# Second-layer weights: half of them converted in the fourth chunk, straight into their kept tiles

## Chip, cores and metric

One NeuronCore of a Trainium2 chip runs the whole program. The metric is device time in microseconds, taken from start to end of one execution; a run is repeated and the median is given. The execution that the profiler recorded has a time of its own.

## What is computed

Hash attention over two batches of 768 tokens with 8 heads of 64, then two feed-forward layers over the 1536 tokens (512 wide, 2048 hidden). Cut to what matters:

```python
# attention: a query sees only keys whose 6 hash bits (signs of q @ proj, k @ proj) are the same
scores = scale * q @ k.T;  scores = where(same_bucket, scores, -1e9)
x = softmax(scores) @ v                          # 1536 x 512 after the heads are joined
# first layer
h = maximum(x @ w_in1, 0.0);   x = (h * h) @ w_out1
# second layer
h = x @ w_in2;  g = maximum(h, 0.0) + alpha * minimum(h, 0.0)
out = g @ w_out2
```

The weights come to the chip as the bits of float64 numbers, 8 bytes each; the kernel makes float32 of them itself, and it splits every operand of a large product into a high and a low part (three products for one).

## The kernel before

The 1536 tokens are four chunks of 384. The program does the attention of chunk 0 alone. Then it goes through the first layer's chunks 0 to 3 and the second layer's chunks 0 to 3, each by `feed_forward(l, c, background)`, in 16 steps `f` over the hidden width. One step does `hidden` (12 matmuls of 384 columns, lines 665 to 667), the activation (lines 672 to 683, giving a high part `gh` and a low part `gl`) and `project` (9 matmuls of 512 columns, lines 693 to 697) for the step before. The attention of chunks 1 to 3 runs beside the first layer's chunks 0 to 2.

A *unit* `(l, f, o)` is one weight tile of 128 x 512: `o` is 0 for the matrix into the hidden width and 1 for that out of it, so a layer has 32 units. How a unit comes to TensorE:

- `load_bits` (lines 578 to 582) loads its 512 KB of float64 bits into a buffer `wide`.
- `to_f32` (584 to 599) makes float32: one ScalarE copy of the high word into `we` (line 591), and on VectorE two instructions that build sign and low bits in `wsg` (593, 594) and one that joins them (596). `we` and `wsg` have one buffer each. The result goes into the tile that is handed over, or else stays in `we`.
- `split_w` (612 to 619) makes the high part `wh` on ScalarE (617) and the low part `wl` on VectorE or GpSimd (618).

The first layer's units are converted in chunk 0 by `fetch` (631 to 649), written to DRAM, and fetched again in each later chunk. The second layer's 32 units are converted by `ahead` (601 to 605): `to_f32` without a tile, then a DMA of 256 KB from `we` to a DRAM tile `w_d[u]` (line 605). Later `keep` (607 to 610) loads each from DRAM into a tile of the pool `res` that stays until the end, so that the second layer fetches nothing. In that layer `fetch` finds a unit in `kept` and takes it from there (634, 635).

Work beside the feed-forward is a list of steps with marks: `Background` (554 to 568) is called at 80 slots of a chunk and runs as many steps as its marks ask for at that place, laid evenly between two marks. The list of `load_bits` and `ahead` has 64 steps between 1.0 and 2.9 chunks (lines 797 to 802), that is beside chunks 1 and 2 of the first layer. The list of `keep` has 32 steps between 0.25 and 1.3 chunks counted from the start of chunk 3 (819, 820). Chunk 3 begins after the attention's pools are closed and the weight pools opened again with more buffers (812 to 816): `wide` has three buffers before and eight after.

All these DMAs are issued by SyncE's queue in the order that the compiler fixed. The compiler places each engine's instructions by the order in which they were written and by its own reckoning of when their operands are ready, so an instruction can stand ahead of one that was written earlier.

Of the kernel before, what the change touches and what calls it, by code (L numbers as in the profile page):

```python
# [23 lines left out]
EVICT = ("aavaav", "avavav", "vvavva", "vvavva")  # L24

LEAD = 0.88


@with_exitstack
def kernel(  # L30
# [20 lines left out]
    nc = tc.nc  # L51
# [10 lines left out]
    KFF = w_in1.shape[0]  # L62
# [438 lines left out]
    def attention_beside():  # L501


        pairs = [Pair(c, j) for c in range(1, NCH) for j in range(NPAIR)]
        steps, ends = [], []

        def begin():
            if (1, 0) not in raw:
                load_pair(1, 0)

        def turn(pr, u):
            for a in range(2):
                steps.append(lambda a=a: pr.p_t(*divmod(u, NTB), a))

        def values(pr, part):
            steps.append(lambda: pr.av(part))

        def finish(pr):
            steps.append(pr.finish)
            if pr.j == NPAIR - 1:  # L520
                ends.append(len(steps))

        steps += [begin] + pairs[0].prepare()
        last = 2 * NTB - 1
        for n, pr in enumerate(pairs):
            old = pairs[n - 1] if n else None
            prep = pairs[n + 1].prepare() if n + 1 < len(pairs) else []
            for u in range(2 * NTB):
                steps.append(lambda pr=pr, u=u: pr.scores(*divmod(u, NTB)))
                if prep and u != 1:  # L530
                    steps.append(prep.pop(0))
                if u == 0 and old:
                    turn(old, last)
                    steps.append(old.recip)
                    values(old, 0)
                if u == 1 and old:
                    values(old, 1)
                    values(old, 2)
                if u:
                    turn(pr, u - 1)  # L540
                if u == 4 and prep:
                    steps.append(prep.pop(0))
                if u == (3 if old and old.j == NPAIR - 1 else last) and old:
                    finish(old)
            assert not prep
        turn(pr, last)
        steps.append(pr.recip)
        for part in range(3):
            values(pr, part)
        finish(pr)  # L550
        return steps, ends
# [22 lines left out]
    w_d = {}  # L574
    kept = {}
    y_d = {}

    def load_bits(u):
        l, f, o = u
        t = state["wide"].tile([P, DM, 2], U32, tag="wide", name="wbits")  # L580
        nc.sync.dma_start(out=t.rearrange("p n b -> p (n b)"), in_=(WO if o else WI)[l][f].bitcast(U32))
        w_bits[u] = t

    def to_f32(u, w=None):


        if u not in w_bits:
            load_bits(u)
        t = w_bits.pop(u)
        e = state["conv"].tile([P, DM], F32, tag="we", name="we")  # L590
        nc.scalar.activation(e, t[:, :, 1].bitcast(F32), AF.Copy, scale=2.0 ** -112)
        s = state["conv"].tile([P, DM], U32, tag="wsg", name="wsg")
        nc.vector.tensor_scalar(s, t[:, :, 1], 0x80000000, None, ALU.bitwise_and)
        nc.vector.scalar_tensor_tensor(s, t[:, :, 0], 29, s, ALU.logical_shift_right, ALU.bitwise_or)
        w = e if w is None else w
        nc.vector.scalar_tensor_tensor(  # L596
            w.bitcast(U32), e.bitcast(U32), 3, s, ALU.logical_shift_left, ALU.bitwise_or
        )
        return w

    def ahead(u):

        w = to_f32(u)
        w_d[u] = dram.tile([P, DM], F32, tag="w%d_%d_%d" % u, name="w%d_%d_%d" % u)
        nc.sync.dma_start(out=w_d[u], in_=w)

    def keep(u):

        kept[u] = state["res"].tile([P, DM], F32, name="w%d_%d_%d" % u)
        nc.sync.dma_start(out=kept[u], in_=w_d[u])  # L610

    def split_w(u, engine):
        w = w_f.pop(u)
# [142 lines left out]
    def second_x(c):  # L756

        cell = []

        def begin():  # L760
            new_x((1, c))
            y = state["res"].tile([P, NTB, DM], F32, tag="yb", name="yb")
            nc.sync.dma_start(out=y, in_=y_d[c])
            cell.append(y)

        def block(t):
            ps = ps_s.tile([P, 2, 512], F32, tag="s", name="s")[:, t % 2, :]
            for m in range(KDM):
                nc.tensor.transpose(ps[:, m * P:(m + 1) * P], cell[0][:, t, m * P:(m + 1) * P], ident)
            src = ps.rearrange("p (m n) -> p m n", m=KDM)  # L770
            xh, xl = xT[1, c]
            hi = xh[:, :, t * P:(t + 1) * P]
            nc.scalar.activation(hi, src, AF.Copy)
            nc.vector.tensor_tensor(xl[:, :, t * P:(t + 1) * P], src, f32(hi), ALU.subtract)

        return [begin] + [lambda t=t: block(t) for t in range(NTB)]
# [18 lines left out]
    steps, ends = attention_beside()  # L795
    following = Background(steps, [(0.0, 0)] + [(c + LEAD, n) for c, n in enumerate(ends)])
    steps = []
    for f in range(KFF):
        for o in range(2):
            steps += [lambda u=(1, f, o): load_bits(u), lambda u=(1, f, o): ahead(u)]  # L800

# [14 lines left out]
    state["attention"] = False  # L816


    steps = [lambda f=f, o=o: keep((1, f, o)) for f in range(KFF) for o in range(2)]
    conversion = Background(steps, [(0.25, 0), (1.3, len(steps))])  # L820
    for n in range(NCH + 1):
        steps = second_x(n) if n < NCH else []
# [76 lines left out]
```

## Time and profile before

| | us |
|---|---|
| three timed runs | 833.96, 840.73, 841.98 |
| their median | 840.73 |
| the profiled execution | 836.36 |
| its span, first to last instruction | 834.6 |
| TensorE matmuls busy in the span | 796.7 (95%) |
| VectorE busy | 499.6 (60%) |
| ScalarE busy | 472.4 (57%) |
| GpSimd busy | 360.8 (43%) |

The profiled execution is one run of the program; its span leaves out 1.8 us around the first and last instruction. Times below are in us from the span's start. In the rows PE is TensorE, PEld its weight loads, DVE VectorE, ACT ScalarE, POOL GpSimd, SP SyncE; L596 is line 596 of the kernel. Matmuls are pipelined and their ends are modelled, so an engine that is busy all the time may still be late. A "<-" behind an instruction names what ended the wait before it. The chain of waits is followed back from the last instruction to whatever released it.

### The profile page before, as it was taken

Reading aid. Unit: us, or ns where it says so; the run is one execution under the profiler, and the core shown is the slowest. Engines: PE = TensorE matmul, PEld = TensorE weight load, DVE = VectorE, ACT = ScalarE, POOL = GpSimd, SP = SyncE. Lnnn points to the kernel's source line nnn. Section 1 sums busy time; section 2 is a strip of 40 time slices with the busy share of each in tenths; the row PEclk is TensorE's granted clock in tenths of the full one; section 3 lists DMA queues with packets and bytes.
Section 4 is the critical chain, followed back from the end, with each engine's and each line's share of the span. In section 5 each row is a group of like instructions: output and inputs, shape, how many; then the busy total and the mean of one; then the engine's idle time right before and its main releaser. Section 6 shows DMA issues by size and latency. Waiting matters only on the chain.

```text
span 834.6 us, 12635 instructions
## 1 busy us (share of the span) xinstructions
PE 796.7 (95%) x4384; PEld 646.4 (77%) x4384; DVE 499.6 (60%) x822; ACT 472.4 (57%) x926; POOL 360.8 (43%) x321
## 2 busy tenths in 40 slices
PE   6999899999999999999999999999999999999997
PEld 4665667766777768668787789989988998998995
DVE  7678799978657648687797432234445444444442
ACT  5677677866656556656675466654444444443441
POOL 1002223332455556543333345555455555545553
PEclk9999999999999999999999999999999999999999
DMA  6757678877777776787774499500100001001001
GB/s 183 201 155 235 209 242 257 269 224 207 208 235 223 215 239 215 257 272 230 219 239 145 124 308 330 199 39 1 38 15 24 6 34 38 1 1 38 1 1 38
DMA packets 54864, 127.62 MB, mean 153 GB/s; under 512 B 7216, under 2 KB 11600, under 8 KB 54800
## 3 DMA queue, kind: packets, MB, share of 16 engines
q1 hardware_dynamic: 54800, 126.81, 48.9%
q8 instruction: 34, 0.56, 0.3%
q14 instruction: 30, 0.25, 0.1%
HBM read 82.93 MB, written 23.12 MB: 127 GB/s over the span
## 4 chain that ended last, share of the span: by engine, by line
PE 53%; DVE 4%; DMA 3%; ACT 3%; issue 2%; POOL 1%; POOLq 0%; DVEq 0%; SPq 0%; ACTq 0%
PE acc L697 8%; PE acc L693 8%; PE acc L694 7%; PE m L667 4%; PE m L665 4%; PE m L666 4%; PE h L665 4%; PE h L666 3%; PE h L667 3%; PE m L423 3%; DMA w<-we 2%; PE s L384 2%; PE m L407 2%; DVE we L596 1%; DVE low L389 1%
## 5 line engine op out<-in xcount | busy, mean ns | idle before, releaser
L683 POOL TENSOR_TENSOR gl<-g,gh 128x384 fp32r<-128x384 f32 x128 | 134.6, 1051 | 249.6 <-ACT gh L682 123.0
L693 PE MATMUL acc<-wh,gh 128*128 128x512 f32 x384 | 159.9, 416 | 0.0
L618 POOL TENSOR_TENSOR wl<-wf,wh 128x512 fp32r<-128x512 f32 x80 | 109.2, 1367 | 114.8 <-ACT wh L617 98.2
L694 PE MATMUL acc<-wl,gh 128*128 128x512 f32 x384 | 151.9, 396 | 0.0
L617 ACT ACTIVATE wh<-w 128x512 fp32r<-128x512 f32 x128 | 80.5, 629 | 80.9 <-PE m L666 44.6
L617 ACT ACTIVATE wh<-wf 128x512 fp32r<-128x512 f32 x128 | 80.2, 629 | 68.3 <-PE h L666 35.9
L697 PE MATMUL acc<-wh,gl 128*128 128x512 f32 x384 | 113.8, 396 | 1.8 <-POOL gl L683 1.8
L665 PE MATMUL h<-xh,wh 128*128 128x384 f32 x296 | 107.0, 361 | 2.5 <-ACT xh L451 1.6
L666 PE MATMUL h<-xl,wh 128*128 128x384 f32 x296 | 100.4, 339 | 0.6 <-POOL xl L452 0.6
L667 PE MATMUL h<-xh,wl 128*128 128x384 f32 x296 | 100.6, 340 | 0.0
L389 DVE TENSOR_REDUCE low<-s 128x1 f32<-128x768 f32 x84 | 79.9, 951 | 27.2 <-PE s L384 26.4
L392 ACT ACTIVATE sm<-s,low 128x768 f32<-128x768 f32 x84 | 75.5, 898 | 34.0 <-DVE low L389 33.5
L407 PE MATMUL m<-ident,sm 128*128 128x128 f32 x531 | 85.3, 276 | 3.8 <-ACT q L317 1.3
L384 PE MATMUL s<-k,q 128*128 128x384 f32 x336 | 79.7, 356 | 9.6 <-ACT sm L392 8.3
L697 PEld LDWEIGHTS acc<-wh,gl 128*128 128x128 f32 x384 | 71.9, 188 | 21.0 <-POOL gl L683 4.4
L618 POOL TENSOR_TENSOR wl<-w,wh 128x512 fp32r<-128x512 f32 x64 | 82.7, 1292 | 6.0 <-ACT wh L617 6.0
L693 PEld LDWEIGHTS acc<-wh,gh 128*128 128x128 f32 x384 | 72.2, 188 | 13.2 <-issue 3.1
L407 PEld LDWEIGHTS m<-ident,sm 128*128 128x128 f32 x531 | 65.2, 141 | 21.6 <-ACT q L317 2.5
L682 ACT ACTIVATE gh<-g 128x384 fp32r<-128x384 f32 x64 | 33.5, 524 | 81.6 <-DVE g L681 81.6
L680 DVE TENSOR_SCALAR r<-m,alpha_sb 128x384 f32<-128x384 f32 x43 | 26.5, 617 | 87.0 <-PE m L667 86.8
L384 PEld LDWEIGHTS s<-k,q 128*128 128x128 f32 x336 | 58.2, 192 | 26.4 <-ACT sm L392 16.1
L694 PEld LDWEIGHTS acc<-wl,gh 128*128 128x128 f32 x384 | 72.5, 189 | 7.7
(117 smaller groups left out, 1423.4 us busy)
## 6 DMA issues: line engine op xcount, KB each, us to landing
wf<-w SPq DMA_DIRECT2D x96, 256.0 KB, 3.0
wbits<-in_w_in_dram SPq DMA_DIRECT2D x32, 512.0 KB, 4.2
wbits<-in_w_out_dram SPq DMA_DIRECT2D x32, 512.0 KB, 4.3
q<-q SPq DMA_DIRECT2D x48, 192.0 KB, 3.6
w<-wf SPq DMA_DIRECT2D x32, 256.0 KB, 2.2
w<-we SPq DMA_DIRECT2D x32, 256.0 KB, 2.9
w<-w SPq DMA_DIRECT2D x32, 256.0 KB, 4.7
k<-kh SPq DMA_DIRECT2D x14, 384.0 KB, 4.6
```

Of the source, the lines that this page charges most:

```text
L384: nc.tensor.matmul(ps[:, a, 0:HALF], self.q[:, h, i, qs], self.k[:, h, i, ks], start=i == 0, stop=i == 1)
L389: low_ins = nc.vector.tensor_reduce(low, ps[:, 0:2, 0:HALF], AX.XY, ALU.max, negate=True)
L407: nc.tensor.transpose(ps[:, i * P:(i + 1) * P], pp[:, b * P:(b + 1) * P], ident)
L617: nc.scalar.activation(hi, w, AF.Copy)
L618: engine.tensor_tensor(lo, w, f32(hi), ALU.subtract)
L665: nc.tensor.matmul(hp, wih[:, ks], xh[:, kk, :], start=first, stop=False)
L666: nc.tensor.matmul(hp, wih[:, ks], xl[:, kk, :], start=False, stop=False)
L667: nc.tensor.matmul(hp, wil[:, ks], xh[:, kk, :], start=False, stop=last)
L683: nc.gpsimd.tensor_tensor(gl, g, f32(gh), ALU.subtract)
L693: nc.tensor.matmul(acc[:, t, :], gh[:, blocks[t]], woh, start=first, stop=False)
L694: nc.tensor.matmul(acc[:, t, :], gh[:, blocks[t]], wol, start=False, stop=False)
L697: nc.tensor.matmul(acc[:, t, :], gl[:, blocks[t]], woh, start=False, stop=last)
```

## The change

The list beside chunks 1 and 2 has only the units of the first `AHEAD` = 8 of 16 hidden steps, so 16 units and 32 steps, between the same marks. In the later list each unit has its `keep`, and those of the hidden steps 8 to 15 a `load_bits` ahead of it: 48 steps between the same marks. `keep` loads a unit from DRAM if it is there, and else converts it with `to_f32`, whose last VectorE instruction writes into the kept tile.

```diff
@@ -24,6 +24,8 @@
 LEAD = 0.88
+
+AHEAD = 8
@@ -607,7 +609,10 @@
     def keep(u):
 
         kept[u] = state["res"].tile([P, DM], F32, name="w%d_%d_%d" % u)
-        nc.sync.dma_start(out=kept[u], in_=w_d[u])
+        if u in w_d:
+            nc.sync.dma_start(out=kept[u], in_=w_d[u])
+        else:
+            to_f32(u, kept[u])
@@ -795,7 +800,7 @@
     steps = []
-    for f in range(KFF):
+    for f in range(AHEAD):
         for o in range(2):
             steps += [lambda u=(1, f, o): load_bits(u), lambda u=(1, f, o): ahead(u)]
@@ -816,7 +821,12 @@
-    steps = [lambda f=f, o=o: keep((1, f, o)) for f in range(KFF) for o in range(2)]
+    steps = []
+    for f in range(KFF):
+        for o in range(2):
+            if f >= AHEAD:
+                steps.append(lambda u=(1, f, o): load_bits(u))
+            steps.append(lambda u=(1, f, o): keep(u))
     conversion = Background(steps, [(0.25, 0), (1.3, len(steps))])
```

## Rows read from the trace of the kernel before

**Rows 1.** Table by stage: stretch, length, busy us (instructions) of PE, PEld, DVE, ACT, POOL, clock, DMA share, GB/s

```profile
232.00:368.00 136.00, 130.06 (x754) 98.90 (x753) 90.50 (x140) 81.82 (x167) 76.92 (x66) 1.00 0.74 231
368.00:484.00 116.00, 114.48 (x630) 88.02 (x629) 81.50 (x134) 67.69 (x136) 41.30 (x35) 1.00 0.65 203
484.00:554.00 70.00, 68.36 (x346) 61.03 (x345) 16.11 (x23) 44.17 (x87) 37.47 (x33) 1.00 0.68 232
620.00:689.00 69.00, 68.65 (x350) 61.62 (x349) 31.27 (x53) 29.56 (x52) 36.52 (x32) 1.00 0.07 24
```

**Rows 2.** Chain of waits, 340 to 412 us: start, length, what (pieces at pace)

```profile
350.62 0.69 PE s L384 x4
...
352.35 0.65 PE m L407 x6
...
364.39 0.30 PE m L235 x6
...
368.80 1.44 PE m L423 x8
```

**Rows 3.** Groups of PE, 368 to 484: instruction xcount | busy, mean ns | idle before

```profile
L407 PE MATMUL m<-ident,sm 128*128 128x128 f32 x108 | 17.8, 273 | 0.2 <-ACT q L317 0.2
```

**Rows 4.** Waits of PE, 217 to 368: us in total, times, longest

```profile
PE s L384 <- ACT sm L392: 2.0, 2, 1.0
PE s L251 <- ACT sm L392: 1.5, 1, 1.5
PE s L384 <- DVE kr L275: 1.2, 2, 0.9
PE m L407 <- ACT q L317: 1.1, 1, 1.1
```

**Rows 5.** Waits of PE, 368 to 484, the largest of three groups

```profile
PE s L384 <- ACT sm L392: 0.8, 3, 0.3
```

**Rows 6.** Chain of waits, 340 to 366 us

```profile
340.04 1.68 DVE wsg L594
...
356.78 4.95 DMA w<-we
...
361.84 0.52 ACT we L591
...
362.41 0.98 ACT sm L392 x2
...
363.44 0.96 PE s L384 x4
```

**Rows 7.** Waits of SP's queue, 217 to 368, the largest group

```profile
SPq L605 <- DVE we L596: 33.0, 11, 6.7
```

**Rows 8.** Groups of the conversion's instructions, 233 to 368

```profile
L596 DVE SCALAR_TENSOR_TENSOR we<-we,wsg 128x512 uint32<-128x512 uint32 x16 | 14.0, 876 | 1.8 <-ACT we L591 1.1
L594 DVE SCALAR_TENSOR_TENSOR wsg<-wbits,wsg 128x512 uint32<-128x512 uint32 x16 | 13.8, 861 | 0.3
L591 ACT ACTIVATE we<-wbits 128x512 f32<-128x512 f32 x17 | 11.4, 669 | 9.9 <-DMA wbits<-in_w_in_dram 6.0 <-DMA w<-we 4.0
L593 DVE TENSOR_SCALAR wsg<-wbits 128x512 uint32<-128x512 uint32 x16 | 9.8, 615 | 9.7 <-DMA wbits<-in_w_in_dram 8.3 <-DMA wbits<-in_w_out_dram 1.4
```

**Rows 9.** Waits of ACT for the conversion: 217 to 368, then 368 to 484

```profile
ACT we L591 <- DMA wbits<-in_w_in_dram: 6.0, 3, 3.2
...
ACT we L591 <- DMA w<-we: 9.2, 7, 2.8
```

**Rows 10.** Timeline, 564 to 574: start, length, engine, instruction [idle before]

```profile
568.49 0.53 ACT L682 ACTIVATE gh<-g 128x384 fp32r<-128x384 f32 x1 [1.26 <-DVE g L681]
...
570.76 0.39 PE L693 MATMUL acc<-wh,gh 128*128 128x512 f32 x1
```

**Rows 11.** GpSimd's `gl`: 233 to 368 as a group, 484 to 554 min/median/max

```profile
L683 POOL TENSOR_TENSOR gl<-g,gh 128x384 fp32r<-128x384 f32 x16 | 17.3, 1081 | 0.9
...
L683 POOL TENSOR_TENSOR gl<-g,gh x16: 1003/1017/1021, 488.1 to 551.2; 128x384 fp32r<-128x384 f32 x16
```

## The prediction

> **What bounds the kernel now.** Read the stages first, then what lies above their floor, then who causes it. The table by stage [rows 1] has the second and third chunk of the first layer (232 to 368 and 368 to 484 us), the fourth chunk (484 to 554) and, as a yardstick, the second chunk of the second layer (620 to 689). TensorE is busy in 95% or more of each and its granted clock is 1.00 in all of them, the upper of its two levels (2.4 GHz), so the clock plays no part. A busy PE can still be late. The yardstick chunk is feed-forward alone and takes 69 us; the fourth chunk, without attention too, takes 70. The second chunk also carries one chunk's attention (24 score tiles, 24 x 6 transposes, 12 groups of 8 value products). At the steady pace of the pieces in [rows 2] that is 24 x 0.70 + 24 x 0.65 + 12 x 1.44 = 49.7 us; with 64 small hash products, at 0.30 us for six 3 us, the floor is 69 + 50 + 3 = 122 us against 136 taken: 14 us above it. In the third chunk 108 of the 144 transposes are left [rows 3], and I take the same three quarters for the scores and all the value products: 12.6 + 11.7 + 17.3 + 69 = 111 us against 116, so 5 us above. The fourth chunk and the second layer have 1 us or less. So all that can be won beside the conversions is 14 + 5 = 19 us, and most of it is in the second chunk.
>
> Who causes it: TensorE's own waits in the second chunk are for ScalarE's exponentials and query rows and for VectorE's key rows; the four largest groups come to 5.8 us [rows 4]. In the third the largest group is 0.8 us [rows 5]. The rest of the 19 us is in gaps too small to be listed. The chain of waits shows how a conversion comes into it [rows 6]: the write of a converted tile to DRAM takes 4.95 us, only then may ScalarE start the next tile's conversion (there is one buffer `we`), and behind that conversion on ScalarE's queue stands the exponential for which TensorE waits at 363 us. SyncE is held as well: eleven of those writes wait 33.0 us in all for VectorE in the second chunk [rows 7], and fetches of first-layer weights and copies of q stand behind them on that queue.
>
> **The change, part by part.** *Removed:* for 16 of the 32 units the write `w<-we` and the read back `w<-w`, 256 KB each, so 32 DMAs and 8.4 MB. *Moved:* 16 loads of 512 KB, 16 ScalarE copies and 48 VectorE instructions go from the second and third chunk to the fourth chunk's feed-forward and the start of the second layer. *Added:* no instruction; the last VectorE step writes into the kept tile instead of `we`, and needs no DMA behind it.
>
> *In the second and third chunk.* A unit costs 0.67 us on ScalarE and 0.62 + 0.86 + 0.88 = 2.35 us on VectorE [rows 8]. The 32 units are laid over 1.9 chunks, and after the change 16 units over the same 1.9 chunks, so each of the two stages loses about 8 units: 5.4 us of ScalarE's 82 and 18.8 us of VectorE's 90 in the second chunk, nearly as much in the third. The units now come every 15 us or so instead of 7.5, so the write of one (about 5 us) is over long before the next needs `we`; the waits of `we` for the write, 9.2 us in the third chunk, and for the late load, 6.0 us in the second [rows 9], should nearly vanish. What that is worth to TensorE is bounded by nothing below (score, exponential and transposition still follow each other through the same two engines) and by 19 us above. The nearest rows are TensorE's listed waits, 5.8 + 0.8 = 6.6 us, of which not all come from conversions, while some of the unlisted gaps do. I take 7 us, 5 in the second chunk and 2 in the third.
>
> *In the fourth chunk and after.* The new list has 16 + 32 = 48 steps from 0.25 to 1.3 chunks. At 1.0 there are 48 x 0.75/1.05 = 34 done, so 16 plain loads and 9 conversions fall in the fourth chunk and 7 in the first 0.3 of the second layer's first chunk. VectorE has 16.1 of 70 us busy in the fourth chunk and ScalarE 44.2 [rows 1]; 9 units add 21 and 6 us. TensorE is the cover here: ScalarE and VectorE run ahead of it by the buffers, and the work fits into time in which they wait for it. DMA traffic there hardly changes: the kept tiles' loads fell in that stage; 16 of them (4.2 MB) go and 9 loads of 512 KB (4.7 MB) come, beside 232 GB/s now [rows 1]. In the second layer the cover is thinner. There VectorE makes the activation itself, and its result goes through `gh` to the projection: `gh` ends at 569.02 us and is used at 570.76 [rows 10], so 1.7 us are to spare. Three conversion steps in front of it on VectorE's queue take 2.35 us at the mean of [rows 8], which would be 0.6 us late, for 7 units 4 us if all fall badly; nothing if the order puts them behind it. I take 1 us. The waiting instruction to watch is the ScalarE copy: it waits for the 512 KB load, and `wh`, `gh` of the feed-forward are queued behind it; a wait of the longest kind so far is the 6.0 us in three waits of [rows 9], 3.2 us at most, and the DMA engines are busy in 0.68 of the fourth chunk [rows 1]. The load is issued when one of eight `wide` buffers is free, which is about two units of work ahead, so I count none of it.
>
> The sum is -7 + 1 = -6 us: 836.4 (the profiled execution, its span of 834.6 and 1.8 around it) becomes 830.4. That execution lies 4.4 us below the median of the runs, 840.7; the three runs and it have a mean of 838.3, and I set the change against that mean: 832.
>
> **A rule against it.** VectorE's steps do lengthen when GpSimd works beside them: one `wsg` step took 1.68 us [rows 6] where the mean is 0.86, while GpSimd's `gl` took 1.02 us in the fourth chunk without conversions and 1.08 in the second chunk with them [rows 11]. The Trainium skill, "SBUF — State Buffer", section "Who interferes with whom", says that the two share a pair of ports that is held for a whole instruction, so that the other blocks completely. The trace agrees in that VectorE's steps double, and GpSimd pays 6%. By the rows the moved work costs `gl` 16 x 0.06 = 1 us spread over 16 places, nothing in the sum; by the rule taken strictly it is the slower rival below.
>
> **Rivals.**
> 1. *More comes back: 10 to 14 us.* If the conversions cause most of what lies above the floor in the second chunk (every listed wait there goes through ScalarE or VectorE, the engines relieved), three quarters of the 14 and half of the 5 us go: -12.5 + 1, so 827. For it: [rows 6, 7]. Against it: key rows and exponentials are late in the second chunk for the key preparation too, which stays.
> 2. *Hidden anyway: within 3 us, 838.* TensorE's next wait takes the place of the removed one, since score, maximum, exponential and transposition are a chain of their own. For it: the listed waits are only 6.6 us in 252. Against it: half of VectorE's relief is in the stage that is late.
> 3. *Slower: the conversions hold up the second layer.* One place: VectorE's queue in the second layer's first chunk, three steps of a unit ahead of the activation. Each step that meets GpSimd takes up to 1.68 us [rows 6], a unit 5.0 us, which is 3.3 beyond the 1.7 to spare; 7 units cost 23 us, and with -7 the time is 838 + 16 = 854. It decides against the change from 1 us lost per unit (7 x 1 = 7), and shows as over 1% slower from 2.2 us per unit. For it: 31.3 of VectorE's 69 us are taken there and GpSimd is half busy [rows 1]. Against it: in the second chunk the mean of a unit was 2.35 us with GpSimd busier still, 77 of 136 us.
>
> **How the numbers follow.** One per cent, 8.4 us, is about what a measurement of this kernel can tell from no change; the four times here spread over 8.0 us. The forecast has 0.42, rival 1 has 0.30, rival 2 0.16, rival 3 0.12. Faster by over 1%: rival 1, 0.30. Slower by over 1%: most of rival 3, 0.10. Within: 0.60. The range goes from 824 (838 less the 14 of rival 1) to 841 (rival 2 with the spread of the runs); the upper end leaves out rival 3 and the lower end a twentieth.
>
> **What the changed profile would show.** The second chunk shorter by about 5 us and the third by 2; the write `w<-we` gone from ScalarE's waits; 16 of them and 16 reads `w<-w` left; VectorE 40 us busy in the fourth chunk and still no listed TensorE wait beyond about 1 us there; the first chunk of the second layer within 1 us of the second. The forecast is wrong if TensorE waits for `gh`, `gl` or `wh` in the fourth chunk or after, if ScalarE's copy waits there for `wbits`, or if the second chunk stays at 136 us although its waits for `w<-we` are gone.

## The result: 0.9% slower

| | before | after |
|---|---|---|
| median of 13 runs | 837.98 us | 844.86 us |
| lowest to highest | 833.96 to 842.64 | 841.89 to 848.31 |
| profiled execution, span | 834.6 us | 844.2 us |

The ratio is 1.0086 with an interval of 1.0068 to 1.0105: 7 us more where 6 less were forecast, and above the top of the range, 841. The two profiled executions, from which the stages below are read, lie 9.6 us apart.

From here on a chunk runs from its first hidden matmul to that of the next, so that the chunks of one run add up. "Next" is the first chunk of the second layer, and "late pair" is the fourth chunk of the first layer and that next one together. The table by stage of the kernel before has 135.3, 115.8, 70.7 and 66.2 us for the second, third and fourth chunk and the next (the first three are stages of [rows 1], cut a little otherwise). Its last line, which no row above has, with the columns of [rows 1]:

```profile
554.00:620.20 66.20, 66.20 (x341) 60.11 (x340) 30.29 (x53) 28.62 (x51) 34.00 (x30) 1.00 0.07 24
```

The same four stages of the kernel after, and as a last line the stretch of 6.8 us that is told of below:

```profile
231.60:369.70 138.10, 129.92 (x751) 100.47 (x749) 92.06 (x133) 79.57 (x162) 77.72 (x66) 0.98 0.73 213
369.70:482.40 112.70, 112.70 (x630) 88.05 (x629) 57.21 (x94) 60.33 (x121) 40.80 (x35) 1.00 0.38 114
482.40:559.10 76.70, 69.00 (x342) 60.27 (x341) 45.57 (x59) 50.60 (x99) 37.93 (x32) 0.98 0.78 268
559.10:630.10 71.00, 70.59 (x347) 62.74 (x346) 45.62 (x66) 30.63 (x55) 37.21 (x32) 0.97 0.06 23
556.70:563.50 6.80, 5.38 (x14) 4.36 (x15) 6.49 (x9) 3.12 (x6) 2.69 (x2) 0.50 0.00 0
```

The second chunk is 2.8 us longer, the third 3.1 shorter, the fourth 6.0 and the next 4.8 longer. So in these two executions the early side brought nothing on balance, and the late pair lost 10.8 us. Two views tell why. The first is the same table for the ScalarE copy of the conversion alone (stretch, length, ScalarE busy and number of copies, clock, DMA share, GB/s), first of the kernel before:

```profile
232.20:367.50 135.30, 10.85 (x17) 1.00 0.74 230
367.50:483.30 115.80, 9.91 (x15) 1.00 0.65 204
483.30:554.00 70.70, 0.00 (x0) 1.00 0.68 233
```

and of the kernel after, where the last line is a stretch around the fourth chunk's end:

```profile
231.60:369.70 138.10, 9.43 (x14) 0.98 0.73 213
369.70:482.40 112.70, 0.70 (x1) 1.00 0.38 114
482.40:559.10 76.70, 8.10 (x12) 0.98 0.78 268
559.10:630.10 71.00, 2.67 (x4) 0.97 0.06 23
...
538.60:563.60 25.00, 5.37 (x8) 0.86 0.57 192
```

The sixteen early conversions are not spread over 1.9 chunks: nearly all are done in the second chunk, which has 14 of them where it had 17, and the third has one where it had 15. (One more of each kernel stands just ahead of the second chunk, and a copy on the edge of two stretches is counted in both.) The third chunk has no listed TensorE wait left. The sixteen late ones are drawn together in the same way: eight of them stand in 25 us around the end of the fourth chunk, two in each hidden step. On ScalarE's queue the order that the compiler fixed puts the early ones at 0.81 to 1.94 chunks, where their marks say 1.0 to 2.9, and the late ones at 3.44 to 4.06, where the marks of their part of the list say 3.62 to 4.3.

The second view is what TensorE waits for in the fourth chunk (us in total, times, longest):

```profile
PE acc L698 <- ACT gh L679: 6.5, 3, 3.6
PE m L670 <- ACT wh L622: 0.7, 1, 0.7
PE m L672 <- DVE wl L623: 0.5, 1, 0.5
```

The last two lines are in the kernel before as well. The first line is new, and it is the first layer's own `gh`. ScalarE's timeline in front of it, and VectorE's:

```profile
554.04 0.67 ACT L593 ACTIVATE we<-wbits 128x512 f32<-128x512 f32 x1 [1.15 <-DVE w L598]
554.61 0.62 ACT L622 ACTIVATE wh<-w 128x512 fp32r<-128x512 f32 x1
555.12 0.48 ACT L678 ACTIVATE r<-m 128x384 f32<-128x384 f32 x1
556.99 0.67 ACT L593 ACTIVATE we<-wbits 128x512 f32<-128x512 f32 x1 [1.39 <-DVE w L598]
557.57 0.51 ACT L679 ACTIVATE gh<-r 128x384 fp32r<-128x384 f32 x1
```

```profile
551.35 0.42 DVE L595 TENSOR_SCALAR wsg<-wbits 128x512 uint32<-128x512 uint32 x1
551.81 0.69 DVE L596 SCALAR_TENSOR_TENSOR wsg<-wbits,wsg 128x512 uint32<-128x512 uint32 x1
552.60 1.40 DVE L598 SCALAR_TENSOR_TENSOR w<-we,wsg 128x512 uint32<-128x512 uint32 x1
554.04 1.39 DVE L595 TENSOR_SCALAR wsg<-wbits 128x512 uint32<-128x512 uint32 x1
555.46 0.69 DVE L596 SCALAR_TENSOR_TENSOR wsg<-wbits,wsg 128x512 uint32<-128x512 uint32 x1
556.26 0.69 DVE L598 SCALAR_TENSOR_TENSOR w<-we,wsg 128x512 uint32<-128x512 uint32 x1
556.87 0.68 DVE L623 TENSOR_TENSOR wl<-w,wh 128x512 fp32r<-128x512 f32 x1
```

Between `r` (ready at 555.60) and `gh` stands a conversion's copy. It may write `we` only when VectorE has joined the unit before, at 556.95, and so `gh` begins 1.97 us after `r` was ready, on top of what had been lost in the steps before. VectorE has hardly a gap: two units and one `wl` fill 551.35 to 557.5, 6.1 us. A hidden step of TensorE's own work is 4.18 to 4.19 us; in the kernel before the last products of two successive steps begin at

```profile
538.16 0.69 PE acc L697 x3
542.35 0.69 PE acc L697 x3
```

So in these last hidden steps VectorE, not TensorE, gives the pace. Two of its steps, at 552.60 and 554.04, take 1.40 and 1.39 us, where the same steps of the units beside them take 0.69 and 0.42 us. These two overlap GpSimd's

```profile
552.44 1.02 POOL L688 TENSOR_TENSOR gl<-g,gh 128x384 fp32r<-128x384 f32 x1 [3.42 <-ACT g L681]
553.42 1.73 POOL L623 TENSOR_TENSOR wl<-wf,wh 128x512 fp32r<-128x512 f32 x1
```

During the longest wait, which ends at 558.1 us, the clock falls: the last line of the stage table has 0.50 for 6.8 us, the lower level (1.2 GHz). Of these 6.8 us the wait itself takes 1.4; the 5.4 after it give the work of half their length, 2.7 us less. Of the late pair's 10.8 us, then, 6.5 are more idle time of TensorE (8.1 us against 1.6) and 4.3 more busy time, of which the clock makes 2.7.

### The profile page after: what moved, and what is told of

Read it like the earlier page. It is cut to its first block, busy times and chain, and to the rows that moved or that the text cites. A ratio compares the mean times of both kernels' runs of the same rounds, so it can differ in the third digit from the quotient of the medians.

```text
span 844.2 us, 12567 instructions
## 1 busy us (share of the span) xinstructions
PE 800.8 (95%) x4384; PEld 651.5 (77%) x4384; DVE 517.8 (61%) x822; ACT 471.7 (56%) x926; POOL 364.4 (43%) x321
## 4 chain that ended last, share of the span: by engine, by line
PE 63%; DVE 9%; ACT 4%; DMA 3%; issue 2%; POOL 2%; SPq 0%; POOLq 0%; DVEq 0%; ACTq 0%
PE acc L702 8%; PE acc L698 8%; PE acc L699 8%; PE h L670 5%; PE h L671 5%; PE m L425 5%; PE h L672 5%; PE m L672 4%; PE m L670 4%; PE m L671 4%; PE s L386 3%; PE m L409 3%; DVE wsg L596 2%; DVE wsg L595 2%; POOL wl L623 1%
## 5 line engine op out<-in xcount | busy, mean ns | idle before, releaser
L688 POOL TENSOR_TENSOR gl<-g,gh 128x384 fp32r<-128x384 f32 x128 | 137.5, 1074 | 251.0 <-ACT gh L687 123.0
L698 PE MATMUL acc<-wh,gh 128*128 128x512 f32 x384 | 161.8, 421 | 6.9 <-ACT gh L679 6.5
L698 PEld LDWEIGHTS acc<-wh,gh 128*128 128x128 f32 x384 | 72.8, 190 | 22.8 <-ACT gh L679 7.9
```

Source lines behind the costliest of these rows:

```text
L688: nc.gpsimd.tensor_tensor(gl, g, f32(gh), ALU.subtract)
L698: nc.tensor.matmul(acc[:, t, :], gh[:, blocks[t]], woh, start=first, stop=False)
```

## The experiments

Ratios are to the kernel before on the same chip. The stages are those of one profiled execution of each run, the median is over all its executions (four of e1 and of e7, seven or more of the others). The profiled execution lies up to 4 us from the median: 3.7 below it in e4 (830.89 us), 2.8 below in e8, 4.0 above in e10 (842.98). The late pair took 136.9 us before and 147.7 after.

| run | second | third | fourth | next | median us | ratio (interval) |
|---|---|---|---|---|---|---|
| before | 135.3 | 115.8 | 70.7 | 66.2 | 837.98 to 838.72 | |
| after | 138.1 | 112.7 | 76.7 | 71.0 | 844.86 | 1.0086 (1.0068 to 1.0105) |
| e1_two_we | 135.9 | 112.7 | 76.7 | 75.0 | 848.55 | 1.0109 (1.0073 to 1.0145) |
| e2_hold_late | 137.2 | 112.7 | 72.8 | 75.1 | 845.42 | 1.0072 (1.0051 to 1.0092) |
| e3_hold_both | 129.3 | 114.1 | 72.8 | 75.1 | 839.93 | 1.0002 (0.9979 to 1.0024) |
| e4_no_late | 135.1 | 112.7 | 70.7 | 66.2 | 834.63 | 0.9936 (0.9912 to 0.9961) |
| e5_one_step | 138.6 | 112.7 | 71.0 | 70.5 | 838.98 | 1.0011 (0.9995 to 1.0028) |
| e6_even_late | 129.3 | 114.0 | 79.1 | 66.8 | 834.98 | 0.9959 (0.9943 to 0.9976) |
| e7_three_quarters | 128.8 | 116.9 | 70.7 | 66.1 | 831.22 | 0.9918 (0.9904 to 0.9933) |
| e8_before_held | 136.4 | 115.1 | 70.7 | 66.2 | 837.28 | 0.9996 (0.9978 to 1.0014) |
| e9_no_pool_wl | 136.5 | 112.7 | 71.6 | 70.1 | 838.16 | 0.9990 (0.9967 to 1.0013) |
| e10_not_held | 137.0 | 116.4 | 73.9 | 66.1 | 838.95 | 1.0023 (1.0000 to 1.0045) |

**Only the early side.** The late conversions and their loads are taken away; their kept tiles get the first half's weights from DRAM instead, so half of the second layer's weights is left out.

```diff
-        if u in w_d:
-            nc.sync.dma_start(out=kept[u], in_=w_d[u])
-        else:
-            to_f32(u, kept[u])
+        l, f, o = u
+        nc.sync.dma_start(out=kept[u], in_=w_d[l, f % AHEAD, o])
...
-            if f >= AHEAD:
-                steps.append(lambda u=(1, f, o): load_bits(u))
```

> The changed kernel without the sixteen late conversions: the kept tiles of hidden steps 8 to 15 are loaded from the DRAM tiles of steps 0 to 7, so that part of the second layer's weights is left out and all kept tiles come by DMA. This leaves the early side of the change alone. Theory A: fourth chunk and next return to 137 us together as in the kernel before, second and third chunk stay as in the changed kernel (138 and 113), so the whole is 833 to 836, at most 4 us below the kernel before. If the late loss has another source (the pools lie elsewhere, the order of the fourth chunk's fetches), it stays: 143 us or more together, the whole above 840.

Measured: 834.63 us, ratio 0.9936, and the late pair is at 136.9 us to the tenth. So the whole late loss comes from the late conversions with their loads: by the medians the change loses 844.9 - 834.6 = 10.2 us by them, and its early side alone gains 0.6%, 4 to 5 us. Of the stages the third chunk shows 3.1 us of that, the second next to nothing; 1.8 us lie ahead of the second chunk, where the twelve runs differ by 4 us among themselves. The second chunk took 135.1 us and not the 138 that were expected: it has no half-clock stretch here, of which the last section tells.

**A second buffer for the copy.**

```diff
-        state["conv"] = pool(f"conv{late}", 1, stack)
+        state["conv"] = pool(f"conv{late}", 1 + late, stack)
```

> The changed kernel with two buffers instead of one for `we` and `wsg` after the fourth chunk begins. Theory A (order on ScalarE's queue): in the fourth chunk the compiler packs two conversions into each hidden step, the ScalarE copy into the only `we` waits for VectorE's last step of the unit before, and `gh` stands behind it, so TensorE waits three times for `gh` (1.5, 1.7 and 3.8 us) and then runs 6.8 us at half clock. With a second buffer the copy waits no more: the fourth chunk and the one after it take 137 to 139 us together instead of 147.8, and the whole is about 835. Theory B (VectorE's capacity): a unit costs VectorE about 3 us beside GpSimd, two of them and the split need 6.1 us against 4.2 us of a hidden step, so a second buffer is full after one unit and the waits come back: 143 us or more, the whole 841 to 845.

Measured: 848.55 us, the late pair 151.7 us, more than either theory had. My own first theory, the order on ScalarE's queue with one `we`, fell. ScalarE's and VectorE's timelines at the same place (two lines with "x2" hold two units in a row):

```profile
553.70 0.67 ACT L593 ACTIVATE we<-wbits 128x512 f32<-128x512 f32 x1 [2.39 <-DVE w L598]
554.27 0.51 ACT L679 ACTIVATE gh<-r 128x384 fp32r<-128x384 f32 x1
```

```profile
549.19 2.67 DVE L595 TENSOR_SCALAR wsg<-wbits 128x512 uint32<-128x512 uint32 x2
551.78 1.28 DVE L596 SCALAR_TENSOR_TENSOR wsg<-wbits,wsg 128x512 uint32<-128x512 uint32 x2
552.99 0.68 DVE L598 SCALAR_TENSOR_TENSOR w<-we,wsg 128x512 uint32<-128x512 uint32 x1
```

With two buffers the compiler packed more units into the fourth chunk (all but two, 14 where it had 12), and the copy waits for VectorE as before, here 2.39 us instead of 1.39. The run changes the order along with the buffer, so what the buffer alone does stays open; it does not help where the engine behind it is late on the average.

**Late conversions kept at their written place.** The ScalarE copy is put behind the `gh` of the hidden step beside which it was written.

```diff
-            nc.scalar.activation(gh, r, AF.Square)
+            state["gh"] = nc.scalar.activation(gh, r, AF.Square)
...
-            to_f32(u, kept[u])
+            with tc.issue_after(state["gh"].ins):
+                to_f32(u, kept[u])
```

> The changed kernel, with each late conversion's ScalarE copy kept behind the `gh` of the hidden step beside which it was written, so that the compiler cannot draw conversions of the second layer's first chunk into the fourth chunk. On ScalarE's queue they now lie from 3.62 to 4.25 chunks (3.44 to 4.06 before), about one to two per hidden step. Theory A (packing): the waits for `gh` go or become single ones under 1 us, no half-clock stretch follows, fourth chunk and next 138 to 141 us together, the whole about 836. Theory C (contention: VectorE's conversion steps and GpSimd's `gl` and `wl` slow each other wherever they meet, or the loads of 512 KB crowd the queue): the same work costs the same, 146 us together, the whole 843 to 846.

Measured: 845.42 us; the late pair 147.9 us, as in the changed kernel. The loss only moved: half of the conversions now stand in the second layer's first chunk, and TensorE's largest listed wait from 476 to 632 us is

```profile
PE acc L699 <- ACT gh L688: 5.0, 2, 2.5
```

with `gh` now that of the second layer. In front of the second of these waits VectorE has three steps of one unit ahead of the activation:

```profile
577.47 1.24 DVE L595 TENSOR_SCALAR wsg<-wbits 128x512 uint32<-128x512 uint32 x1
578.74 1.67 DVE L596 SCALAR_TENSOR_TENSOR wsg<-wbits,wsg 128x512 uint32<-128x512 uint32 x1
580.51 1.60 DVE L598 SCALAR_TENSOR_TENSOR w<-we,wsg 128x512 uint32<-128x512 uint32 x1
582.03 0.60 DVE L686 TENSOR_SCALAR r<-h,alpha_sb 128x384 f32<-128x384 f32 x1
```

4.5 us for one unit, all three steps lengthened. Holding alone does not help here. The list itself asks for one conversion in 0.7 of a hidden step and starts only at 0.62 of the fourth chunk, which is the likely reason; the runs with other lists below bear on it.

**How much is VectorE's time.** Each late conversion has one VectorE step instead of three (sign and low bits are left out of these weights); loads and copies stay.

```diff
+        if short:
+            nc.vector.tensor_scalar(w.bitcast(U32), e.bitcast(U32), 3, None, ALU.logical_shift_left)
+            return w
...
-            to_f32(u, kept[u])
+            to_f32(u, kept[u], True)
```

> The changed kernel with one VectorE instruction instead of three in each late conversion: sign and low bits of these sixteen units are left out, so their weights are not exact; loads, ScalarE copies and their places (3.44 to 3.94 chunks) stay as in the changed kernel. Theory E (VectorE's time is what is missing in the late stages: three steps, about 2.9 us beside GpSimd, twice in a hidden step): VectorE has room, `we` is free in time, the fourth chunk and the next take 137 to 139 us together instead of 147.8, the whole 834 to 836. Theory F (ScalarE's copies, the 512 KB loads, or their packing as such): the waits for `gh` stay, 145 us or more, the whole 843 to 846.

Measured: 838.98 us, the late pair 141.5: 6.2 of the 10.8 us go with two of VectorE's three steps, 4.6 stay. Between the two theories, and nearer to the first. What stays is, above all, one wait of 2.4 us for `gh` at 553 us and a half-clock stretch behind it. Its cause was not separated further. The copies are packed more tightly than before, 14 in the fourth chunk and ten in 22.2 us; two of them with `wh`, `wh`, `r`, `gh` and `g` make 4.1 of the 4.19 us of a hidden step by their sum (ScalarE was busy 10.7 of 13.6 us there). And the chain of waits to this place goes back through copies and VectorE steps in turn, on the one `we`, to a load of 512 KB that took 6.25 us.

**How much is GpSimd's part in VectorE's time.** GpSimd's `wl` is left out in the late pair (the projection takes `wh` in its place, so the low part of those weights is left out); VectorE's work is all there.

```diff
+        if not state["attention"] and engine is nc.gpsimd and late():
+            nc.scalar.activation(hi, w, AF.Copy)
+            w_split[u] = (hi, hi)
+            return
```

> The changed kernel with GpSimd's `wl` left out in the fourth chunk and in the second layer's first chunk: the projection there takes `wh` in place of `wl`, so it has the same products but a wrong low part. VectorE's and ScalarE's work is all there, and the places of the conversions are the same (3.44 to 4.06 chunks). If VectorE's steps double because GpSimd works beside them, a unit falls from 2.9 us to about 2.1 in these stages (`gl` is still there), two of them and the split take 4.9 us instead of 6.1, and the fourth chunk and the next take 141 to 144 us together instead of 147.8; the whole 838 to 841. If GpSimd has no part in it, they take 147 us and the whole is 844 to 846.

Measured: 838.16 us, the late pair 141.7 us. The groups of VectorE's three steps from 520 to 570 us, in the changed kernel

```profile
L598 DVE SCALAR_TENSOR_TENSOR w<-we,wsg 128x512 uint32<-128x512 uint32 x14 | 13.3, 951 | 1.4
L596 DVE SCALAR_TENSOR_TENSOR wsg<-wbits,wsg 128x512 uint32<-128x512 uint32 x14 | 12.6, 901 | 0.4
...
L595 DVE TENSOR_SCALAR wsg<-wbits 128x512 uint32<-128x512 uint32 x13 | 9.8, 754 | 2.1 <-DMA wbits<-in_w_in_dram 1.7 <-DMA wbits<-in_w_out_dram 0.2
```

and without `wl` on GpSimd

```profile
L598 DVE SCALAR_TENSOR_TENSOR w<-we,wsg 128x512 uint32<-128x512 uint32 x15 | 14.9, 993 | 1.5
L596 DVE SCALAR_TENSOR_TENSOR wsg<-wbits,wsg 128x512 uint32<-128x512 uint32 x15 | 10.4, 693 | 0.5
...
L595 DVE TENSOR_SCALAR wsg<-wbits 128x512 uint32<-128x512 uint32 x15 | 6.7, 444 | 2.4 <-DMA wbits<-in_w_in_dram 1.2 <-DMA wbits<-in_w_out_dram 1.1
```

A unit falls from 2.61 to 2.13 us, and the late pair is 6.0 of the 10.8 us shorter, as expected if VectorE's steps lengthen beside GpSimd. (The run frees GpSimd's time too; what that alone does was not tried.) The rule that the prediction weighed (the Trainium skill, "SBUF — State Buffer", "Who interferes with whom") is borne out for VectorE in its direction: its steps lengthen where GpSimd works. In its sum the prediction had counted what GpSimd loses and left VectorE's lengthening to rival 3. The two gains, 6.2 and 6.0 us, can't be added: each brings VectorE nearer to where it keeps up.

**Early conversions kept at their written place too.**

```diff
-        w = to_f32(u)
+        with tc.issue_after(state["gh"].ins):
+            w = to_f32(u)
```

> As the run before, and the sixteen early conversions held behind `gh` in the same way, so that they lie from 1.06 to 2.81 chunks on ScalarE's queue instead of all from 0.81 to 1.94. This is the spreading on which the prediction counted. Theory A: half of the second chunk's conversions are now really gone, the second chunk takes 131 to 133 us instead of 138, the third 113 to 115 instead of 112.7, the whole is about 831 to 833. Theory D (the second chunk is held up by key rows and the softmax chain, whoever else is on VectorE): the second chunk stays at 135 us or more and the whole at 836 to 839.

Measured: 839.93 us, no change against the kernel before and above both theories, with the late pair still at 147.9. But the second chunk took 129.3 us (nine conversions), the third 114.1 (seven): 243.4 against 251.1 us, 7.7 us gained. So the price on which the prediction counted for the early side, 7 us, was right once the conversions really are spread. Its mechanism shows as well: ScalarE's waits of `we` for the write and for the late load, 4.0 and 6.0 us in the second chunk before and 9.2 in the third, are gone: its copies of both chunks start without any wait. How much of the 7.7 us they made, and how much VectorE's relief, was not separated.

**The holding alone.** The kernel before, with its 32 early conversions held in the same way.

> The kernel before, with all 32 conversions held behind `gh` as in the runs above; they lie from 1.00 to 2.88 chunks, where they lay from 0.81 to 2.69. If the second chunk gains from having half the conversions, this one keeps its 135 us and the whole is 836 to 839. If it was the holding itself that gave 8 us in the run with both held, the second chunk takes 130 us here too and the whole is 830 to 833.

Measured: 837.28 us, ratio 0.9996, second chunk 136.4 us, with 17 conversions as before. Holding as such brings nothing; having half the conversions in the second chunk does.

**Late conversions evenly over the fourth chunk.** Both held, and the late list reordered.

```diff
-    for f in range(KFF):
-        for o in range(2):
-            if f >= AHEAD:
-                steps.append(lambda u=(1, f, o): load_bits(u))
-            steps.append(lambda u=(1, f, o): keep(u))
-    conversion = Background(steps, [(0.25, 0), (1.3, len(steps))])
+    for f in range(AHEAD):
+        for o in range(2):
+            steps.append(lambda u=(1, AHEAD + f, o): load_bits(u))
+            steps.append(lambda u=(1, AHEAD + f, o): keep(u))
+            steps.append(lambda u=(1, f, o): keep(u))
+    conversion = Background(steps, [(0.05, 0), (0.95, len(steps))])
```

> The held kernel (early conversions spread from 1.06 to 2.81 chunks) with the late list in another order: each conversion followed by one load from DRAM, from 0.05 to 0.95 of the fourth chunk, so that one conversion falls on each hidden step of that chunk (3.06 to 3.94) and none on the second layer. Theory E: VectorE needs 0.7 + 3.0 = 3.7 us of 4.2 per hidden step, just enough; the fourth chunk takes 71 to 73 us, the next 66 to 67, the whole is 831 to 834. Theory F or loads that crowd the queue (21 MB in 70 us there, 300 GB/s): the fourth chunk takes 75 us or more and the whole is 836 or more.

Measured: 834.98 us, ratio 0.9959; the late pair 145.9. The next chunk is nearly whole again at 66.8 us, but the fourth takes 79.1, against theory E and on the side of the other (75 us or more). TensorE's largest listed waits are

```profile
PE m L674 <- DVE wl L625: 2.7, 1, 2.7
PE acc L700 <- ACT gh L681: 1.9, 1, 1.9
```

and the chain of waits at the chunk's start has

```profile
471.48 5.67 DMA wbits<-in_w_in_dram
...
479.83 1.20 DVE wl L625
...
481.07 0.69 PE m L674
```

The first conversion's load took 5.67 us; VectorE stood waiting for it, and behind it on VectorE's queue the `wl` that TensorE needed. The chunk's mean granted clock is 0.94: half-clock stretches at the two long waits do most of the rest. VectorE was busy 66.8 us in the chunk, and 16 hidden steps of 4.19 us are 67: one conversion per hidden step is just about what it can do, and leaves no room for a late load.

**Three quarters early, one quarter late.** Both held, 24 early units (8 in the second chunk, 16 in the third), 8 late ones over the fourth chunk.

```diff
-AHEAD = 8
+AHEAD = 12
...
-Background(steps, [(1.0, 0), (NCH - 1.1, len(steps))])
+Background(steps, [(1.0, 0), (2.0, 16), (NCH - 1.1, len(steps))])
...
+            for k in range(3):
+                steps.append(lambda u=(1, 3 * f + k, o): keep(u))
+    conversion = Background(steps, [(0.1, 0), (0.95, len(steps))])
```

> Held conversions, 24 early ones with 8 in the second chunk and 16 in the third, and 8 late ones spread over the fourth chunk (3.12 to 3.88), one in two hidden steps. Theory E: VectorE has 0.7 + 1.5 us of work per hidden step in the fourth chunk, so it and the next take 137 to 138 us; second chunk 129 to 131, third 115 to 117; the whole 830 to 833. Theory F: the late stages lose half of what they lose in the changed kernel, 142 us together, the whole 835 to 837.

Measured: 831.22 us, ratio 0.9918 (0.9904 to 0.9933): faster than both kernels, and every stage within 0.2 us of where theory E put it. Its stages:

```profile
232.80:361.60 128.80, 126.68 (x750) 98.31 (x749) 76.79 (x115) 76.19 (x156) 77.78 (x66) 1.00 0.67 194
361.60:478.50 116.90, 113.99 (x629) 88.00 (x628) 88.14 (x136) 68.59 (x136) 43.06 (x35) 1.00 0.63 199
478.50:549.20 70.70, 69.06 (x349) 61.70 (x348) 39.24 (x47) 48.20 (x95) 40.90 (x33) 1.00 0.77 265
549.20:615.30 66.10, 66.10 (x340) 60.10 (x339) 30.31 (x53) 28.61 (x51) 34.13 (x30) 1.00 0.07 24
```

Eight conversions in the fourth chunk cost TensorE nothing, though VectorE's steps there are as long as ever (3.04 us a unit), and no stage has a half-clock stretch.

**The same without holding.** The two holds are taken out again.

> The kernel with 24 early and 8 late conversions, without the holding behind `gh`: the compiler again draws the early ones forward (sixteen by 2.0 chunks and all by 2.44) and the late ones a little (3.00 to 3.69). If the place of the conversions decides, the second chunk is back at 135 us or more instead of 128.8, the third takes 113 to 115 instead of 116.9, the late stages 137 to 138, and the whole is 835 to 838. If holding has no part in the 831 us, it stays at 830 to 833.

Measured: 838.95 us, the second chunk at 137.0 (14 conversions instead of eight), the third at 116.4, the late pair at 140.0. The third and the late pair are 1 and 2 us over the expectation, in a profiled execution that is 4 us above the median. Without the holds the compiler draws the conversions together and the gain is gone. It is their place that counts, and the number in each stage.

## Why the prediction was wrong, step by step

*What bounds the kernel: right.* The second chunk is where time can be won. e3 and e7 took 6.0 and 6.5 us out of it, the third fell from 115.8 to 112.7 without conversions, which is 2 us from the floor worked out from [rows 2, 3].

*"The 32 units are laid over 1.9 chunks, and after the change 16 units over the same 1.9 chunks": this step failed.* The marks of a list say where its steps are written, and the compiler puts each engine's instructions in an order of its own. Beside the second chunk it used the room that was freed for the units that had been due later, so the stage that was late kept 14 of 17 conversions, and the stage with 5 us to give lost 14 of its 15. (That it did so is read from the queues; why was not tried.) The front part had the sign of it: it says that the compiler can place an instruction ahead of one written earlier. I took the written spacing for the real one all the same. The price for a really spread list (7 us) was right: e3 measured 7.7 in these two stages. In the changed kernel the early side was worth 4 to 5 us by e4, more than its stages show.

*"16 plain loads and 9 conversions fall in the fourth chunk and 7 in the first 0.3 of the next" and "the work fits into time in which they wait for it": this step failed, and it costs more.* Twelve conversions fell in the fourth chunk, eight of the late ones in 25 us at two per hidden step. The cover was reckoned over the stage (16.1 + 21 of 70 us for VectorE, measured 45.6), where it holds; it had to be reckoned over a hidden step, where two units of 2.61 us and a `wl` of 0.7 make 5.9 us against 4.19. At the prediction's own 2.35 us a unit the sum is 5.4 us, so it fails there without any lengthening. The term taken at +1 us was 10.8 in the profile. About 6 us go with VectorE's work or with GpSimd beside it (e5, e9); what makes the other 4 to 5 was not taken apart. And e2 shows that holding the copies at their written places moves the loss without lessening it.

*Rival 3 had the mechanism, but neither its place nor its weight.* Three steps of a unit on VectorE's queue, lengthened by GpSimd, hold up an activation: that is what e2 shows in the second layer, at the very place that the rival named, with a unit of 4.5 us. In the changed kernel the place was the fourth chunk, by way of `we` and ScalarE's queue, which the prediction had counted as covered. It had 0.12; the argument against it (a mean of 2.35 us in a stage with GpSimd busier) says nothing of a stage in which units follow each other without a gap.

*The wait for `wbits` was rightly counted as nothing in the changed kernel.* In the fourth chunk ScalarE waited 2.1 us in two for these loads, and VectorE 5.0 us in two, before 527 us, where TensorE lost nothing; in the packed steps behind it VectorE waited for none. In e6, where the list starts with the chunk, it came as described, on VectorE instead of ScalarE.

*"The clock plays no part": right of the profiled execution of the kernel before, wrong of the kernel after.* Two stretches at half clock, 6.8 us each, begin inside a wait; what lies behind the wait (6.2 and 5.4 us) takes 3.1 and 2.7 us. One of them stands in the second chunk, and without it that chunk would have been 135.0 us, about as before. No term of the sum had a price for what follows a wait. Nor was the profiled execution a fair sample: its mean granted clock is 0.997, while the executions of the kernel before that were run beside the experiments have 0.990 to 0.998, on the mean 0.994, and those of the kernel after 0.987 to 0.993, on the mean 0.990. As an estimate from these means, 0.4% of 840 us, some 3 of the 7 us between the medians can go by way of the clock.

*The range* went up to 841 on the ground that the late work is covered. It left out rival 3, which the prediction itself priced at up to 23 us (854).

## What to carry to other kernels

Work that is moved under a bound engine is covered only if it fits into each period of that engine, step by step and at the rate at which the compiler will place it; a stage's mean says little. A list with marks is a wish: look at where the instructions stand on their queues, and tie them to something of the period (here behind `gh`) where their spacing is the point. And where two engines slow each other, price the loss of both: the one with the least to spare decides.

## What the runs showed of the hardware

TensorE's clock fell in the middle of the kernel; the profiled execution of the kernel before has no half-clock stretch between 93 us and its last 1 us. In the changed kernel the first such stretch begins in the 2.8 us wait at 285 to 288 us, the second in the 3.6 us wait that ended at 558 us:

```profile
287.10:293.90 6.80, 6.16 (x28) 5.46 (x28) 4.15 (x8) 2.17 (x5) 2.20 (x2) 0.50 0.71 221
```

In the other runs stretches of 3.4 and 6.8 us stand in or behind single waits of 1.9 to 2.8 us, one of 10.2 us at two waits of 3.7 and 2.2 us (e1), and one of 3.4 us behind two waits of 0.7 and 1.1 us close together (e10, at 492 us). It is not certain to follow: e4 has the same wait of 2.8 us at the same place, and its clock stays at 1.00:

```profile
286.50:293.30 6.80, 6.21 (x44) 4.89 (x44) 5.77 (x10) 3.33 (x8) 2.93 (x2) 1.00 0.72 213
```

So one wait of 3 us may cost 3, or it may cost 6. What decides between the two was not tried.
